# Fused sparse attention and two-of-four expert attention: four-quarter strided values, long-run loads, another split of the tokens, projections of the first batch in parts, other shifts of the steps

## Chip, core and metric

The kernel runs on one core of one Trainium2 chip, as one program that is launched once. The metric is device time in microseconds (us). Before the change the median of 3 runs was 509.25 us (508.88 to 509.28).

## What is computed

Eight batches of 576 tokens. In a first stage 8 heads of 64 channels attend: heads 0 to 3 to the last 32 tokens ("local"), heads 4 to 7 to all earlier tokens with the same remainder modulo 32 ("strided"; 18 tokens per remainder). The result, 512 channels per token, is the input x of a second stage with four experts, each a causal attention of one head of 64 channels with its own projections; every token takes the two experts (K = 2) with the highest gate logits.

Here `rel` is query minus key position and `stride` is 32.

```python
mask_local = (rel >= 0) & (rel < stride)
mask_strided = (rel >= 0) & (pos[None, :] % stride == pos[:, None] % stride)
...
for e in range(E):
    q = x @ wq[e]
    k = x @ wk[e]
    v = x @ wv[e]
    scores = scale * (q @ k.transpose(0, 2, 1))
    scores = np.where(causal, -1000000000.0, scores)
    ...
    ye = a @ v @ wo[e]
    for kk in range(K):
        mask = topk[:, :, kk] == e
        out += mask[..., None] * w[:, :, kk:kk + 1] * ye
```

## The kernel before

**Stage 1** (`stage1(b, hp)`, once for each batch b and pair of heads hp; hp 0 and 1 are local, 2 and 3 strided). It loads q and k of the pair (`load_qk`: L395 local, L401 strided) and v (`load_v`: L422 and L425 local, L430 and L433 strided), all on SyncE's queue (SP). A strided block g holds 54 tokens, those of three remainders (18 tokens each); there are 10 such blocks and one of 36. TensorE (PE) transposes the blocks (`tp`, L446), multiplies queries by keys (`s`, L475), a softmax runs over VectorE (DVE), GpSimd (POOL) and ScalarE (ACT) (L489 to L511), PE transposes the probabilities (`pt`, L534 local, L536 strided) and multiplies them by the values (`xa`: L560 local, L565 strided). The result is split into a high and a low part in a reduced float format (`xh` L580, `xl` L582), so that a product of float32 precision can be had from three faster matmuls (`split3`).

For the strided values of before, the matmul of head h takes its rows from partitions 64h and its output to partitions 64h: two quarters of the 128 x 128 array are used. For the strided scores the rows follow the head and the output the half hf, so all four quarters are.

**Stage 2**: per batch and pair of experts ep, `project` (L674) makes q and k, `values2` (L621) the values and gate logits, and `attend(b, ep, qk, un, key)` runs twice (un = 0 and 1). Queries are cut into five tiles, the first of 64 tokens and four of 128 (`QT`). Per tile: scores against all keys up to the tile's end (`s2`, L727; the 64-token tile in quarters, L709, against 128 keys), row minimum of the negated scores (`max2`, L738, L712), exponential (`exp2`, L745, L715), scaling by the gate weight (`scale2`, POOL, L768, L762), transposes in blocks of 128 keys (`t2`, L790, L795), copies of those (`t2_out`), the product with the values (`acc`, L826, L815), a split (`oh`, `ol`, L840, L842), and the output projection (`out_tile`, `yp`, L857) and a store (L869). The two 64-token tiles of neighbouring batches share one output tile.

**The order of the work** is made by a list scheduler in the program (`schedule`, L160). Each step is an `op(kind, engine, key, ...)`, with a key that is roughly its wanted time; the table `PRI` adds a shift for the kind, and for the kind in a batch. Of the steps that can start at the same time, the one with the lowest key goes first; for PE a step in another mode (how the array is divided: whole, two row halves, two column halves, quarters) has `MODE_PEN = 5.0` added. Each engine's queue runs in the order that comes out. PSUM's 8 banks and the buffers in SBUF are rings.

Of batch 0's `project`, each step of 12 matmuls reads x of all four pairs of heads, so it follows all of stage 1 of that batch:

```python
op("pj", {"PE": 12 * 0.134}, key + step * u, mm, r=xbufs(b) + wbufs(nm), w=[pj, qk[j, u]], mode=M128)
```

Of the kernel before, what the change touches and what calls it, by code (L numbers as in the profile page):

```python
# [20 lines left out]
def attention_moe_kernel(  # L21
# [28 lines left out]
    QT = [(0, 64), (64, 128), (192, 128), (320, 128), (448, 128)]  # L50
    UNITS = [(0, 320, [0, 1, 2]), (320, 256, [3, 4])]
# [29 lines left out]
    class Ring:  # L81
# [30 lines left out]
        "lo_w": -10.0, "lo_w 0": -8.0, "load_qk": -4.0, "load_qk 0": -6.0, "load_qk 7": 6.0, "load_v": 3.0,  # L112
        "load_v 0": -2.0, "load_v 7": 18.0, "load_w": -1.0, "load_w 0": 6.0, "mask 0": -1.0, "mask 7": 15.0,
# [12 lines left out]
        "yp_out": 18.0, "yp_out 0": -9.0, "yp_out 7": 10.0,  # L126
    }

    def op(kind, eng, key, fn, r=(), w=(), mode=None, npk=0, after=()):
# [3 lines left out]
        o.key = key + PRI.get(kind, 0.0) + PRI.get(f"{kind} {batch[0]}", 0.0)  # L133
# [154 lines left out]
    m_str = const.tile([128, 6, 54], F32, name="m_str")  # L288
    m_cau = const.tile([128, S], F32, name="m_cau")
    m_first = const.tile([128, 128], F32, name="m_first")  # L290
    for m in (m_loc, m_str, m_cau, m_first):
        nc.vector.memset(m, 0.0)
# [9 lines left out]
    for hf in range(2):  # L302
        for sl, off in ((slice(0, 5), 0), (slice(5, 6), 10 if hf else 0)):
            v_ = m_str[64 * hf:64 * hf + 64, sl].rearrange("p i (g u) -> p i g u", u=NJ)
            n_ = sl.stop - sl.start
            keep(v_, [[0, n_], [-NJ, 3], [-1, NJ]], -off, 1)
            keep(v_, [[0, n_], [NJ, 3], [0, NJ]], NJ - 1 + off, -1)
    keep(m_cau[:, S - 128:], [[-1, 128]], 0, 1)
    for hf in range(2):
        keep(m_first[64 * hf:64 * hf + 64], [[-1, 128]], 0, 1)  # L310
# [49 lines left out]

    P2 = [ring(f"p2{t}", [128, 128] if t == 0 else [128, 2, q0 + m], 2) for t, (q0, m) in enumerate(QT)]
    NAT = ring("nat", [128, 11 * 2 * D], 2)
    QKT = ring("qkt", [128, 2, S], 2)
    VR = ring("v1", [128, 9 * 2 * D], 2)
    PL = ring("p1l", [128, 2, 5, 96], 2)
    PSR = fixed("p1s", [128, 6, 2, D], 2, value=lambda t: [t[:, :, h, 54:] for h in range(2)])
# [6 lines left out]
    def stage1(b, hp):  # L373
# [5 lines left out]
        nat = (P2[NT - 1] if b == 0 and local else NAT).new(f"nat_{n}")  # L379
# [6 lines left out]
        def nv():  # L386
            if local:
                t = nat.t.rearrange("p a c -> p (a c)") if b == 0 else nat.t
                return t[:, :9 * 2 * D].rearrange("p (g h d) -> p g h d", h=2, d=D)
            return nat.t.rearrange("p (g h d) -> p g h d", h=2, d=D)  # L390
# [12 lines left out]
        for h in range(2):  # L403
            for src, p0 in ((q, 0), (k, 64)):
                op("load_qk", {"SP": 0.66 if local else 1.15}, (k0 - 30 if b else hp), lambda e, src=src, p0=p0, h=h: load_qk(e, src, p0, h),
                   w=[nat], npk=576)

        def vv():
            if local:
                return vt.t[:96].rearrange("p (g h d) -> p g h d", g=9, h=2)  # L410
            return vt.t[:, :11 * D].rearrange("p (g d) -> p g d", d=D)

        def pv2():
            if local:
                return ptt.t[:96].rearrange("p (h f i c) -> p h f i c", h=2, f=2, i=5)
            return ptt.t[:, :12 * 64].rearrange("p (f i c) -> p f i c", f=2, i=6)

        def load_v(e, h):
# [7 lines left out]
            else:  # L426
                for r in range(3):
                    ap = bass.AP(tensor=base.tensor, offset=base.offset + r * D,
                                 ap=[[STR * D, NJ], [3 * D, 10], [1, D]])
                    dma.dma_start(vv()[64 * h + NJ * r:64 * h + NJ * r + NJ, 0:10, :], ap)  # L430
                ap = bass.AP(tensor=base.tensor, offset=base.offset + 29 * D,
                             ap=[[D, 3], [STR * D, NJ], [1, D]])
                dma.dma_start(vv()[64 * h:64 * h + 54, 10, :], ap)  # L433


        for u, (g0, g1) in enumerate(((0, SPL), (SPL, NG))):
            tp = [RB.new(f"tp{u}{x}_{n}") for x in "qk"]
            ws = [GW if local or g < 10 else 36 for g in range(g0, g1)]
            cn, c0 = sum(ws), g0 * GW

            def tps(e, tp=tp, g0=g0, ws=ws):
                c = 0
                for g, w_ in enumerate(ws, g0):
                    for x in range(2):
                        r = slice(64 * x, 64 * x + w_)
                        nc.tensor.transpose(tp[x].t[:, c:c + w_], nv()[r, g].rearrange("p h d -> p (h d)"),  # L446
                                            ident[r, r])
                    c += w_

            op("tp", {"PE": 0.058 * len(ws) + 0.03}, k0 - 14 + u, tps, r=[nat], w=[*tp, qkt], mode=MR)  # L450
            for x in range(2):
                op("tp_out", either(cn), k0 - 13 + u, lambda e, t_=tp[x], x=x, c0=c0, cn=cn: copy(
                    e, qkt.t[:, x, c0:c0 + cn], t_.t[:, :cn]), r=[tp[x]], w=[qkt])

        for h in range(2):
            op("load_v", {"SP": 1.0 if local else 1.9}, (k0 - 25 if b else 4.0 + hp), lambda e, h=h: load_v(e, h), w=[vt], npk=864 if local else 594)
# [8 lines left out]
        def scores(e):  # L465
            for i in range(ni):
                for hf in range(2):
                    g = i + hf * (ni - 1)
                    if local:
                        q0, c0 = 64 * g, max(64 * g - STR, 0)  # L470
                    else:
                        q0, c0 = (54 * g, 54 * g) if g < 10 else (S - 64, S - 54)
                    for h in range(2):
                        r = slice(64 * h, 64 * h + 64)
                        nc.tensor.matmul(sp[h].t[64 * hf:64 * hf + 64, nk * i:nk * i + nk],  # L475
                                         qkt.t[r, 0, q0:q0 + 64], qkt.t[r, 1, c0:c0 + nk], start=True, stop=True)
# [3 lines left out]
        msk = m_loc if local else m_str  # L480

        def pv():
            return p.t if local else p.t.rearrange("p i h c -> p h i c")[:, :, :, :nk]
# [42 lines left out]
        for u in range(2 if local else 1):  # L526
            pt = [RB.new(f"pt{u}{hf}_{n}") for hf in range(2)]

            def tps2(e, pt=pt, u=u):
                for i in range(ni):  # L530
                    for hf in range(2):
# [3 lines left out]
                        else:  # L535
                            nc.tensor.transpose(pt[hf].t[:, 64 * i:64 * i + 64],  # L536
                                                p.t[r, i].rearrange("p h c -> p (h c)"), ident[r, r])

            op("pt", {"PE": 0.06 * ni + 0.03}, k0 - 2 + 0.5 * u, tps2, r=[p[u]] if local else [p[0], p[1]], w=[*pt, ptt], mode=MR)
            for hf in range(2):  # L540
                def dst(u=u, hf=hf):
                    return (pv2()[:, u, hf] if local else pv2()[:, hf]).rearrange("p i c -> p (i c)")
# [383 lines left out]
```

## Time and profile before

| | |
|---|---|
| median of 3 runs | 509.25 us (508.88 to 509.28) |
| the profiled execution's own time | 508.14 us |
| its span, first to last instruction | 506.4 us |
| PE busy | 487.6 us (96%) |
| DVE, ACT, POOL busy | 342.0, 298.5, 205.5 us |
| mean granted TensorE clock | 0.983 of full speed |
| DMA | 43.53 MB, 133,856 of 138,803 packets under 512 B |

The page gives busy time by engine; a table of stretches gives the same in chosen windows with the granted clock; the chain of waits that ended last gives, for pieces of work on the path, their start and the time until the next piece. Float32 matmuls stand in the trace as two instructions each.

### The profile page before, as it was taken

Reading aid. Unit: us, or ns where it says so; the run is one execution under the profiler, and the core shown is the slowest. Engines: PE = TensorE matmul, PEld = TensorE weight load, DVE = VectorE, ACT = ScalarE, POOL = GpSimd, SP = SyncE. Lnnn points to the kernel's source line nnn. Section 1 sums busy time; section 2 is a strip of 40 time slices with the busy share of each in tenths; the row PEclk is TensorE's granted clock in tenths of the full one; section 3 lists DMA queues with packets and bytes.
Section 4 is the critical chain, followed back from the end, with each engine's and each line's share of the span. In section 5 each row is a group of like instructions: output and inputs, shape, how many; then the busy total and the mean of one; then the engine's idle time right before and its main releaser. Section 6 shows DMA issues by size and latency. Waiting matters only on the chain.

```text
span 506.4 us, 17970 instructions
## 1 busy us (share of the span) xinstructions
PE 487.6 (96%) x7192; PEld 411.9 (81%) x7192; DVE 342.0 (68%) x1033; ACT 298.5 (59%) x831; POOL 205.5 (41%) x257
## 2 busy tenths in 40 slices
PE   4779999999999999999999999999999999999997
PEld 3678887998779987898879987799878888788864
DVE  4764888658685778666786687766687677844460
ACT  2653668647765467645665566754676467744462
POOL 6753456520634244441555135352263415520440
PEclk9769999999999999999999999999999999999999
DMA  7759643512451143611542323531344212100103
GB/s 138 164 112 191 132 94 85 133 27 65 119 132 45 37 101 101 170 35 39 136 107 56 73 64 100 148 83 26 92 124 109 49 24 69 45 22 1 54 33 104
DMA packets 138803, 43.53 MB, mean 86 GB/s; under 512 B 133856, under 2 KB 133856, under 8 KB 138720
## 3 DMA queue, kind: packets, MB, share of 16 engines
q1 hardware_dynamic: 138720, 42.39, 35.4%
q8 instruction: 57, 0.93, 0.8%
q14 instruction: 26, 0.21, 0.1%
HBM read 32.92 MB, written 9.44 MB: 84 GB/s over the span
## 4 chain that ended last, share of the span: by engine, by line
PE 88%; SPq 4%; DVE 2%; DMA 2%; ACT 1%; issue 1%; POOL 1%; POOLq 0%; ACTq 0%; DVEq 0%
PE bank L674 20%; PE bank L621 11%; PE bank L857 11%; PE bank L826 10%; PE bank L727 9%; PE bank L790 6%; PE bank L475 5%; PE bank L565 4%; PE bank L446 4%; PE bank L560 4%; PE bank L534 2%; SPq L395 1%; PE bank L709 1%; DMA nat<-in_k_dram 1%; PE bank L536 1%
## 5 line engine op out<-in xcount | busy, mean ns | idle before, releaser
L768 POOL TENSOR_SCALAR p<-p,st,wt 128x192 f32<-128x192 f32 (+3 forms) x128 | 83.4, 666 | 20.2 <-DVE st L752 16.8
L745 ACT ACTIVATE p<-p,st 128x192 f32<-128x192 f32 (+3 forms) x128 | 78.2, 613 | 15.1 <-DVE st L738 14.9
L275 DVE COPY th<-bank 128x384 f32<-128x384 f32 (+2 forms) x87 | 40.0, 476 | 41.1 <-PE bank L790 30.5
L738 DVE CUSTOM_DVE_ANT_0 p<-bank,m_cau 128x192 f32<-128x192 f32 (+3 forms) x128 | 56.2, 476 | 11.5 <-PE bank L727 10.5
L502 POOL TENSOR_TENSOR p1l<-p1l,st 128x960 f32<-128x960 f32 (+1 forms) x18 | 29.0, 1617 | 84.9 <-DVE st L500 60.7
L826 PE MATMUL bank<-th,vs 128*64 128x256 f32 (+1 forms) x512 | 55.3, 356 | 0.0
L727 PE MATMUL bank<-qk 64*128 64x288 f32 (+3 forms) x320 | 54.9, 444 | 0.0
L275 ACT COPY th<-bank 128x384 f32<-128x384 f32 (+2 forms) x105 | 41.6, 420 | 15.3 <-PE bank L790 8.1
L826 PEld LDWEIGHTS bank<-th,vs 128*64 128x64 f32 x512 | 34.4, 137 | 18.2 <-DVE pt L275 1.3
L790 PEld LDWEIGHTS bank<-ident,p 64*128 64x128 f32 x896 | 37.0, 139 | 14.1 <-issue 5.5
L621 PE MATMUL bank<-wh_v,xh 128*128 128x260 f32 (+1 forms) x160 | 46.6, 291 | 0.0
L790 PE MATMUL bank<-ident,p 64*128 64x64 f32 x896 | 45.8, 228 | 0.6 <-POOL p L768 0.5
L621 PE MATMUL bank<-wl_v,xh 128*128 128x260 f32 (+1 forms) x160 | 45.2, 283 | 0.0
L621 PE MATMUL bank<-wh_v,xl 128*128 128x260 f32 (+1 forms) x160 | 45.0, 281 | 0.0
L275 ACT COPY qkt<-bank 128x252 f32<-128x252 f32 (+3 forms) x106 | 37.3, 409 | 12.1 <-PE bank L446 12.1
L275 ACT COPY qk<-bank 128x288 f32<-128x288 f32 x46 | 18.3, 398 | 44.1 <-PE bank L674 43.8
L511 POOL TENSOR_TENSOR p1l<-p1l,st 128x960 f32<-128x960 f32 (+1 forms) x18 | 29.0, 1618 | 29.3 <-DVE st L509 28.9
L674 PE MATMUL bank<-xh,wh_k 128*128 128x288 f32 x128 | 39.8, 311 | 0.0
L674 PE MATMUL bank<-xh,wh_q 128*128 128x288 f32 x128 | 38.5, 301 | 0.0
L674 PE MATMUL bank<-xl,wh_k 128*128 128x288 f32 x128 | 38.0, 297 | 0.0
L674 PE MATMUL bank<-xh,wl_k 128*128 128x288 f32 x128 | 38.0, 297 | 0.0
L674 PE MATMUL bank<-xh,wl_q 128*128 128x288 f32 x128 | 37.7, 294 | 0.0
(125 smaller groups left out, 1219.9 us busy)
## 6 DMA issues: line engine op xcount, KB each, us to landing
out_dram<-ys SPq DMA_DIRECT2D x32, 256.0 KB
v<-in_v_dram SPq DMA_DIRECT2D x32, 192.0 KB
v<-in_v_dram SPq DMA_DIRECT2D x96, 45.0 KB
nat<-in_q_dram SPq DMA_DIRECT2D x28, 144.0 KB
nat<-in_k_dram SPq DMA_DIRECT2D x28, 144.0 KB
nat<-in_q_dram SPq DMA_DIRECT2D x64, 49.5 KB
nat<-in_k_dram SPq DMA_DIRECT2D x64, 49.5 KB
nat<-in_q_dram SPq DMA_DIRECT2D x32, 45.0 KB
```

The lines of the kernel that those rows point to most:

```text
L275: (nc.scalar.copy if e == "ACT" else nc.vector.tensor_copy)(dst, src)
L502: nc.gpsimd.tensor_tensor(P, P, bc[0], ALU.subtract)
L511: nc.gpsimd.tensor_tensor(P, P, bc[2], ALU.mult)
L621: nc.tensor.matmul(vp.t[:m, :NV], xx.t[:, t0:t0 + m], ww.t[:, kt, :], start=i == 0, stop=i == 11)
L674: nc.tensor.matmul(pj.t[:, :HS], ww.t[:, kt, ep * 128:(ep + 1) * 128], xx.t[:, c], start=i == 0, stop=i == 11)
L727: nc.tensor.matmul(sp[a].t[:, :cn], qk.t[r, 0, q0:q0 + m], qk.t[r, 1, c0:c0 + cn], start=True, stop=True)
L738: lambda e, sp=sp, p=p, a=a, c0=c0, cn=cn, hh=hh, nk=nk, acc_=acc_: nc.vector.tensor_tensor_reduce(out=p.t[:, a, c0:c0 + cn], in0=sp[a].t[ ...
L745: op("exp2", {"ACT": 0.485 + 0.00083 * nk}, k_ + 1, lambda e, p=p, a=a, ci=ci: nc.scalar.activation(p.t[:, a], p.t[:, a], AF.Exp, bias=st. ...
L768: lambda e, p=p, a=a, ci=ci, t=t: nc.gpsimd.tensor_scalar(p.t[:, a], p.t[:, a], st.t[:, 14 + ci + a:15 + ci + a], wt.t[:, t, 2 * ep + a:2 ...
L790: nc.tensor.transpose(tp[hf].t[:, 64 * c:64 * c + 64], p2[t].t[r, a, k0:k0 + 128], ident[r, r])
L826: nc.tensor.matmul(acc.t[o, dst:dst + 128 * nb], vw, x.t[:, c:c + nb, :].rearrange("p c q -> p (c q)"), start=j == 0, stop=j == js[-1], sk ...
L857: nc.tensor.matmul(yp.t[:, :DM], xx.t[:, c0:c0 + 128], ww.t[:, ep, :], start=i == 0, stop=i == 5)
```

## The change

- The strided values use row half x = g // 6 and column half h, so four quarters; all 22 matmuls (44 instructions) form one step that writes two banks. For that the probabilities are laid out so that, of each pair of blocks, the two heads lie in opposite halves.
- Strided block g now holds, of each of three runs of 11 (11, 10) neighbouring remainders, one. So one DMA packet carries 10 or 11 tokens of 64 floats for q and k, and 4, 5 or 6 for v, where it carried one; one DMA loads both heads. Per strided pair 6 DMAs for q and k instead of 12, and 6 for v instead of 8. The q and k blocks are transposed by head, 2 x 6 x 2 transposes instead of 22. x is written by three splits instead of two.
- The four 128-token tiles come first, the 64-token tile last: keys 128, 256, 384, 512 and 576 instead of 64 (128 computed), 192, 320, 448 and 576. The last tile runs in quarters, in two halves of 288 keys. In the product with the values it is a third block of 64 columns beside the 128 of tile 3 (`W1 = 192`).
- Batch 0's projections are cut into four steps of three matmuls, one for each pair of heads.
- `PRI` has a shift for nearly every kind in every batch, up to 168.5 in size (before: up to 20).
- Zero fills of the padding of `nat` and `p24`, another mask (`m_last`) instead of `m_first`, a smaller `m_str`.

```diff
-    QT = [(0, 64), (64, 128), (192, 128), (320, 128), (448, 128)]
-    UNITS = [(0, 320, [0, 1, 2]), (320, 256, [3, 4])]
+    QT = [(0, 128), (128, 128), (256, 128), (384, 128), (512, 64)]
+    UNITS = [[0, 1, 2], [3, 4]]
...
-        "acc": 1.0, "acc 0": 8.0, "acc 7": 2.0, "exp2": 1.0, "exp2 0": 10.0, "exp2 7": -4.0, "exp2_0": 15.0,
...
+        "acc": 13.0, "acc 0": -28.0, "acc 1": 0.5, "acc 2": -13.5, "acc 3": 24.0, "acc 4": 4.0, "acc 5": 8.5,
...
+        "gate4 2": 4.5, "gate4 3": 88.5, "gate4 4": -54.5, "gate4 5": 6.5, "gate4 6": 5.5, "gate4 7": 40.5,
+        "gate5": -47.0, "gate5 0": -2.0, "gate5 1": -168.5, "gate5 2": -61.0, "gate5 3": -33.5,
...
                 for r in range(3):
-                    ni = 11 if r < 2 else 10
-                    ap = bass.AP(tensor=base.tensor, offset=base.offset + r * D,
-                                 ap=[[STR * D, NJ], [3 * D, ni], [1, D]])
-                    nc.sync.dma_start(nv()[p0 + NJ * r:p0 + NJ * r + NJ, 0:ni, h, :], ap)
+                    n_ = (11 if r < 2 else 10) * D
+                    ap = bass.AP(tensor=base.tensor, offset=base.offset + 11 * r * D,
+                                 ap=[[STR * D, NJ], [S * D, 2], [1, n_]])
...
-                            r = slice(64 * h, 64 * h + 54)
-                            nc.tensor.matmul(xa.t[o, c:c + z - a], vv()[r, g, :], pv2()[r, hf, i, a:z],
-                                             start=True, stop=True)
...
+                for s_ in range(6):
+                    for x in range(2):
+                        g = 6 * x + s_
+                        if g > 10:
+                            continue
+                        n_ = 54 if g < 10 else 36
+                        m, b_ = divmod(s_, 2)
+                        r = slice(64 * x, 64 * x + n_)
+                        for h in range(2):
+                            nc.tensor.matmul(xa[x].t[64 * h:64 * h + 64, 54 * s_:54 * s_ + n_], vv()[r, h, s_, :],
+                                             pv2()[r, h ^ b_, b_, m, :n_], start=True, stop=True)
...
+            if b == 0:
+                prev = []
+                for kt in range(KT):
...
+                    prev = [op("pj", {"PE": 3 * 0.134}, key + step * u + 0.1 * kt, part,
...
-    BLK = [[[(0, 1), (0, 2), (1, 1), (1, 2), (2, 2)]],
-           [[(0, 3), (0, 4), (1, 3), (1, 4), (2, 3), (2, 4)], [(3, 3), (3, 4), (4, 4)]]]
+    BLK = [[(0, 0), (0, 1), (0, 2), (1, 1), (1, 2), (2, 2)], [(0, 3), (1, 3), (2, 3), (3, 3)]]
...
+            if t == NT - 1:
+                for hh in range(2):
...
+                            nc.tensor.matmul(sp.t[r, :HS], qk.t[r, 0, q0:q0 + 64], qk.t[r, 1, c0:c0 + HS],
+                                             start=True, stop=True)
...
+        jobs = [(a, BLK[un]) for a in range(2)] + ([("l", [(j, NT - 1) for j in range(NT)])] if un else [])
...
+                    if un == 0:
+                        c0, cn, s0 = 128 * j, 384 - 128 * j, 128 * (0, 3, 5)[j]
+                    else:
+                        c0, cn, s0 = 0, W1 if j < 4 else 64, W1 * j
+                    nc.tensor.matmul(acc.t[o, c0:c0 + cn], vw, th[a].t[:, s0:s0 + cn],
```

## Rows read from the trace of the kernel before

**Rows 1.** The page, part 1: busy time and share of the span by engine.

```profile
PE 487.6 (96%) x7192; PEld 411.9 (81%) x7192; DVE 342.0 (68%) x1033; ACT 298.5 (59%) x831; POOL 205.5 (41%) x257
```

**Rows 2.** Busy time in three stretches: window, length, five engines, granted clock, DMA share.

```profile
0.00:53.00 53.00, 39.39 (x633) 35.02 (x634) 30.33 (x78) 24.51 (x64) 29.68 (x50) 0.84 0.75 151
53.00:468.00 415.00, 414.21 (x6256) 351.33 (x6257) 296.63 (x897) 256.08 (x718) 164.35 (x189) 1.00 0.33 80
468.00:507.00 39.00, 34.05 (x308) 25.57 (x306) 15.04 (x58) 17.91 (x49) 11.42 (x19) 1.00 0.18 62
```

**Rows 3.** PE's waits by what released it: total us, times, longest.

```profile
PE bank L446 <- POOL m_first L284: 6.0, 1, 6.0
...
PE bank L790 <- POOL p L768: 0.5, 1, 0.5
```

**Rows 4.** The chain of waits, 112 to 171 us: start, us until the next.

```profile
118.89 1.80 PE bank L727 x12
...
121.89 0.85 PE bank L475 x48
...
127.51 0.80 PE bank L446 x22
128.31 0.36 PE bank L709 x4
...
130.28 0.46 PE bank L790 x10
130.73 0.06 PE bank L795 x2
130.79 0.38 PE bank L727 x4
131.17 0.31 PE bank L790 x10
...
133.93 0.27 PE bank L815 x4
134.19 1.08 PE bank L826 x12
135.28 0.52 PE bank L790 x12
135.79 0.59 PE bank L727 x4
136.39 0.18 PE bank L790 x6
...
140.77 2.10 PE bank L826 x20
...
147.07 1.41 PE bank L565 x44
```

**Rows 5.** The first stretch in parts, columns as in Rows 2.

```profile
0.00:6.00 6.00, 0.04 (x1) 0.07 (x1) 2.46 (x12) 1.28 (x1) 4.84 (x17) 1.00 0.57 123
...
26.00:31.00 5.00, 3.13 (x59) 2.66 (x61) 3.90 (x11) 3.94 (x12) 4.33 (x7) 0.78 0.39 83
31.00:37.00 6.00, 5.39 (x95) 5.09 (x91) 3.19 (x8) 2.42 (x6) 1.49 (x3) 0.50 0.55 123
```

**Rows 6.** The timeline of PE in the first 40 us.

```profile
21.19 1.54 PE L475 MATMUL bank<-qkt 64*64 64x54 f32 x48
...
34.47 2.63 PE L565 MATMUL bank<-pt,v 54*64 54x54 f32 x44 [0.61 <-ACT pt L275]
37.03 0.61 PE L674 MATMUL bank<-xh,wh_k 128*128 128x288 f32 x1
```

**Rows 7.** The timeline of SP, DVE and POOL in the first 14 us.

```profile
2.50 0.32 DVE L260 MEMSET p1s<- 128x60 f32 x4
...
7.76 1.16 SPq L401 DMA_DIRECT2D nat<-in_k_dram  x3
```

**Rows 8.** The timeline of POOL from 200 to 225 us: one unit's scalings.

```profile
213.90 3.04 POOL L768 TENSOR_SCALAR p<-p,st,wt 128x448 f32<-128x448 f32 x4 [0.42 <-DVE st L752]
```

More of the change, by code (lines that the diff above doesn't have):

```diff
@@ L132, in op @@
         o.eng, o.fn, o.mode, o.npk = eng, fn, mode, npk
[L133 removed]
+        o.key = round(key + PRI.get(kind, 0.0) + PRI.get(f"{kind} {batch[0]}", 0.0), 3)
         o.succ, o.ready, o.end = [], 0.0, None
@@ L302, in attention_moe_kernel @@
     for hf in range(2):
[L303 to L307, printed above, removed]
+        v_ = m_str[64 * hf:64 * hf + 64].rearrange("p (g u) -> p g u", u=NJ)
+        keep(v_, [[-NJ, 3], [-1, NJ]], 0, 1)
+        keep(v_, [[NJ, 3], [0, NJ]], NJ - 1, -1)
     keep(m_cau[:, S - 128:], [[-1, 128]], 0, 1)
     for hf in range(2):
-        keep(m_first[64 * hf:64 * hf + 64], [[-1, 128]], 0, 1)
+        keep(m_last[64 * hf:64 * hf + 64, HS - 64:], [[-1, 64]], 0, 1)
     tie = const.tile([128, E, E], F32, name="tie")
@@ L378, in stage1 @@
         k0 = T * (b + 0.25 * hp) if b else 2.0 + 4.0 * hp
-        nat = (P2[NT - 1] if b == 0 and local else NAT).new(f"nat_{n}")
+        nat = (P2[3] if b == 0 and local else NAT).new(f"nat_{n}")
         qkt, st = QKT.new(f"qkt_{n}"), ST1.new(f"st1_{n}")
@@ L451, in stage1 @@
             for x in range(2):
[L452 to L456, printed above, removed]
+                c0 = x * S + 64 * g0 if local else (2 * x + u) * cn
+                op("tp_out", either(cn), k0 - 13 + u, lambda e, t_=tp[x], c0=c0, cn=cn: copy(
+                    e, qkt.t[:, c0:c0 + cn], t_.t[:, :cn]), r=[tp[x]], w=[qkt])
@@ L459, in stage1 @@
+        for h in range(2 if local else 1):
+            op("load_v", {"SP": 1.0 if local else 2.6}, (k0 - 25 if b else 4.0 + hp), lambda e, h=h: load_v(e, h), w=[vt], npk=864 if local else 700)
         sp = [RB.new(f"s{h}_{n}") for h in range(2)]
@@ L586, in attention_moe_kernel, with split @@
-    VS = fixed("vs", [128, NT, NV], 2, value=lambda t: [t[64:128, 0, :]])
+                op("pt_out", either(pn * ni), k0 - 1.5 + 0.5 * u, lambda e, pt=pt, hf=hf, dst=dst, rows=rows, pn=pn: copy(
+                    e, dst(), pt[hf].t[:rows, :64 * ni].rearrange("p (i c) -> p i c", c=64)[:, :, :pn]), r=[pt[hf]], w=[ptt])
+        def split(xa, key, u, *parts):
+            for u, (s_, x_, n_) in enumerate(parts, u):
+                op("xh", {"ACT": act(n_)}, key, lambda e, s_=s_, x_=x_: nc.scalar.copy(x_(xh.t), s_(xa.t)),
+                   r=[xa], w=[xh[u]])
+                op("xl", {"DVE": dve(n_)}, key + 0.5, lambda e, s_=s_, x_=x_: nc.vector.tensor_sub(
+                    x_(xl.t), s_(xa.t), x_(f(xh.t))), r=[xa, xh[u]], w=[xl[u]])
@@ L604, in xbufs @@
     def xbufs(b):
-        return [X[b, kt][i][u] for kt in range(KT) for i in range(2) for u in range(2)]
+        return [X[b, kt][i][u] for kt in range(KT) for i in range(2) for u in range(3)]
     def wbufs(nm):
@@ new lines, in attend, with mm @@
+            sp = [RB.new(f"s2_{n}_{t}_{a}") for a in range(2)]
+            def mm(e, sp=sp, q0=q0, nk=nk):
+                for a in range(2):
+                    r = slice(64 * a, 64 * a + 64)
+                    nc.tensor.matmul(sp[a].t[:, :nk], qk.t[r, 0, q0:q0 + 128], qk.t[r, 1, :nk], start=True, stop=True)
+            op("s2", {"PE": nk * 4 / 2400 + 0.02}, k_, mm,
+               r=[qk[0, u] for u in us] + [qk[1, u] for u in range((nk - 1) // HS + 1)],
+               w=[*sp, p[0], p[1]], mode=MR)
@@ new lines, in attend @@
+            for a in range(2):
+                op("max2", {"DVE": 0.23 + 0.00102 * nk}, k_ + 0.5,
+                   lambda e, sp=sp, p=p, a=a, nk=nk, ci=ci: nc.vector.tensor_tensor_reduce(
+                       out=p.t[:, a, :nk], in0=sp[a].t[:, :nk], in1=m_cau[:, S - nk:], scale=-SCALE, scalar=BIG,
+                       op0=ALU.add, op1=ALU.min, accum_out=st.t[:, ci + a:ci + a + 1]),
+                   r=[sp[a]], w=[p[a], st[t, a]])
+            for a in range(2):
+                op("exp2", {"ACT": 0.485 + 0.00083 * nk}, k_ + 1, lambda e, p=p, a=a, ci=ci, nk=nk: nc.scalar.activation(
+                    p.t[:, a, :nk], p.t[:, a, :nk], AF.Exp, bias=st.t[:, ci + a:ci + a + 1], scale=-1.0,
@@ L835, in attend @@
+                    nc.tensor.matmul(acc.t[o, c0:c0 + cn], vw, th[a].t[:, s0:s0 + cn],
+                                     start=j == 0, stop=j == idx[-1], skip_group_check=True)
+        cols = {0: 768, 1: 4 * W1 + 64}[un]
+        dsts = [O[b, ep]] + ([OF[b // 2, ep]] if un else [])
+        op("acc", {"PE": cols * 4 / 2400 + 0.1}, kk + 4.5, av, r=[vs[j] for j in range(idx[-1] + 1)] + th,
            w=[acc] + [y[un if i == 0 else b % 2] for i, pair in enumerate(dsts) for y in pair], mode=MC)
-        parts = [(O[b, ep], un, 256 * un, 64 - 64 * un, 256)]
@@ L846, in out_tile @@
     def out_tile(b, t, key):
-        c0 = 0 if t == 0 else 128 * (t - 1)
+        last = t == NT - 1
+        c0 = 0 if last else QT[t][0]
         yp, ys = RB.new(f"yp_{b}_{t}"), YS.new(f"ys_{b}_{t}")
-        src = [OF[b // 2, ep] if t == 0 else O[b, ep] for ep in range(2)]
-        need = [x[i] for pair in src for x in pair for i in ((0, 1) if t == 0 else (int(t > 2),))]
+        src = [OF[b // 2, ep] if last else O[b, ep] for ep in range(2)]
+        need = [x[i] for pair in src for x in pair for i in ((0, 1) if last else (int(t > 2),))]
         def mm(e):
```

344 lines of the change are left out of this document (163 added, 181 removed), and 75 rows, old and new, of the table PRI.

## The prediction

> **What bounds the kernel now.** I read the busy time by engine first: PE is busy 96% of the span, the next engine, DVE, 68% [rows 1]. A share over the span can hide stages, so the table of stretches comes next. From 53 to 468 us PE is busy 414.21 of 415 us at the full granted clock, while DVE has 296.63 and DMA a share of 0.33 [rows 2]: there nothing but PE's own work sets the time. PE's waits agree: the longest is 6.0 us at the very start, and the largest one behind POOL's scalings is 0.5 us, once [rows 3]. The two ends are different. In the first 53 us PE is busy 39.39 us at a mean clock of 0.84, in the last 39 us it is busy 34.05 [rows 2]. So the change is to be priced by what it takes from PE's stream, and apart from that at the start.
>
> **Prices.** The chain of waits gives pieces of PE's stream with the time until the next piece, so pipelining is in them. Score pieces of 192 and 320 columns (both heads, two instructions each) last 0.38 and 0.59 us: (0.59 - 0.38) / 128 = 1.64 ns for a column [rows 4]. Ten transposes behind work in another mode last 0.46 us, ten behind work in their own mode 0.31 us [rows 4]: a change of mode costs about 0.15 us.
>
> **Strided values.** 44 instructions in two quarters last 1.41 us, 32 ns each. The strided scores have the same shape (64 x 64, 54 columns) in four quarters: 48 in 0.85 us, 17.7 ns each [rows 4]. 44 x 17.7 ns = 0.78 us, so 0.63 us less per strided pair. From both sides: nothing, if the quarters did not overlap, and 0.70 us if the time were halved. I take the scores' row, since the order there (each row half with both column halves) and the banks (one for each row half) are those of the change. The split of the first bank now waits for all 44 instead of the first 24, but 24/44 of 1.41 is 0.77 us: it starts when it did.
>
> A rule of the Trainium skill speaks against this. TensorE: Matmul & The Clock Gate, section "Wait — 56ns, not 53.3ns?", has it that matmuls start no closer than about 25 ns however few columns they have. By it the 44 would take 1.10 us (an estimate from that page's figure), and the sum below would be 4.3 us smaller. The scores' row, 17.7 ns, is against it for quarters; as a rival it stands below, worked out from rows.
>
> **Strided transposes.** 22 take 0.80 us, 36 ns each [rows 4]; 24 instead: +0.07 us. Together a strided pair saves 0.56 us. There are two per batch; the seven later batches' 14 lie where PE is the bound: 14 x 0.56 = **7.8 us**.
>
> **The other split of the tokens**, for each batch and pair of experts (16 of them), all on PE:
> - Scores. Before 0.36 + 0.38 + 0.59 + 1.80 = 3.13 us for 128 + 192 + 320 + (448 + 2 x 288) = 1664 columns [rows 4]. After 128 + 256 + 384 + 512 + 576 = 1856: 192 more, x 1.64 ns = +0.32 us. The last tile has two pieces in quarters where there was one, which may cost no change of mode or one (0.15): +0.40 us, between 0.32 and 0.47.
> - Transposes. Before 0.46 + 0.06 + 0.31 + 2 x (0.52 + 0.18) = 2.23 us for 58, of which one change of mode is 0.15, so 36 ns each [rows 4]. After 24 + 16 + 10 = 50: -0.28 us.
> - Product with the values. Before 0.27 + 1.08 + 2.10 us for 64 + 640 + 1152 columns [rows 4]; after 768 and 832. 256 columns fewer are 0.42 us; the separate four instructions of the first tile fall away, 0.03 us: -0.45 us.
>
> That is 0.40 - 0.28 - 0.45 = -0.33 us, x 16 = **5.3 us**. The other engines keep about the same sizes (exponentials and scalings of 3200 columns before, 3136 after) and have at least 118 us to spare in the 415 [rows 2], so I cost them at nothing. If that cover were gone, the place would be the transposes behind POOL's scalings, 3.04 us for a unit's four [rows 8].
>
> **Loads.** A strided pair's q and k need 6 DMAs instead of 12, each issue about 1.16 / 3 = 0.39 us of SP's queue [rows 7]; v 6 instead of 8. That is 8 x 0.39 = 3.1 us of SP per pair, and less DMA time, but from 53 us on PE waits for no load, so it is worth nothing there. In batch 0 it puts the weights and batch 1's loads, queued behind, up to 6.2 us earlier. What is late next there is the softmax of the pairs: in the trace the last strided values wait for a copy on ACT, not for a load [rows 6].
>
> **The start.** Batch 0's projections begin at 37.03 us, behind the last strided values (2.63 us, as PE then runs at half its clock) [rows 6]. Three effects:
> - The values in four quarters: the scores' 48 take 1.54 us at that clock [rows 6], so 44 take 1.41: 1.2 us less; for the two pairs, less what falls into gaps, 2.2 us.
> - Projections by pairs: nine of the twelve matmuls of a step no longer need the last pair. From 26 to 37 us PE is idle 1.87 + 0.61 = 2.5 us [rows 5]; filled with such matmuls, that is 2.5 us less to do later. Bounds: 0, if the weights' low parts, made on POOL and DVE in just this stretch, come too late, and 5.7 us if in addition the clock, 0.78 and 0.50 there [rows 5], were full (half of the 6 us at 0.50 and a little more). The parts stand in PE's queue ahead of the last pair's transposes and values; were a part to wait for a weight, those would wait too, up to the 2.5 us again as a loss.
> - The zero fills: eight more at 0.32 / 4 = 0.08 us [rows 7] and a mask of 288 columns, about 0.9 us on DVE, in the first 6 us, in which DVE is busy 2.46 [rows 5]: hidden. If they were not, 0.9 us.
>
> I take **4.7 us** together, between -0.5 and 8.
>
> **The tail** (idle 5 of 39 us [rows 2]) has the same four output tiles behind the last values; I take nothing.
>
> **Sum.** 7.8 + 5.3 + 4.7 = 17.8 us. The profiled execution took 508.14 us (span 506.4 and 1.7 around it): 490.3. The median of the runs is 1.1 us above it: **491.4 us**.
>
> **The rivals.**
> 1. *The quarters overlap in part.* Halfway between 32 and 17.7 ns, 24.9 ns, the 44 take 1.09 us and a pair saves 0.32 - 0.07 = 0.25 us, 3.5 instead of 7.8 in all: **495.7**. For it: the values have 11 blocks, so the last pair of matmuls is alone in its row half, and 54 columns at 1.64 / 2 ns would be 44 ns, so that more than columns counts. Against it: the scores' 17.7 ns. Chance 0.08. The floor of 25 ns of the Trainium skill would give about this time.
> 2. *The quarters don't overlap*, so the change doesn't do what it says: 1.41 us stays and 0.07 is added, 9.8 us of the sum lost at the 14 pairs, less 1 at the start: 491.4 + 8.8 + 1.1 = **501**. It would need a conflict that the scores don't have, such as the values' operands lying in copies of another layout. Chance 0.06.
> 3. *More from the start and fewer changes of mode.* The loads let stage 1 of batch 0 end earlier, the clock rises in it, 8 us instead of 4.7, and the new shifts save 5 changes of mode in a batch (the chain has 17 between 118.89 and 147.07 us, the first and the last of [rows 4], so some 30 in a batch), 40 x 0.15 = 6: **482**. For it: the start's idle time and half clock. Against it: DVE and POOL are busy 3.90 and 4.33 of the 5 us from 26 to 31 [rows 5]. Chance 0.12.
> 4. *The new shifts break up the modes*: slower than before. The shifts are up to 168 where the penalty for another mode is 5, so of PE's waiting steps the key alone decides, and steps of one mode stand less together. Place: PE's stream from 53 to 468 us, which has no slack. Price 0.15 us a change. It cancels the 17.8 us from 119 more changes on, 15 in a batch; with 20 more, **515**. The Trainium skill (TensorEngine Tiling, "Key Properties") also says that a change of mode drains the engine, and the 0.46 against 0.31 us agrees. Against it: the shifts of before, up to 20, also override a penalty of 5, and PE's stream still is dense. Chance 0.10, of which 0.08 ends slower.
>
> **How the numbers follow.** Forecast 0.64; rivals 0.08, 0.06, 0.12 and 0.10 as above. Predicted is the forecast's time, 491.4. The range reaches down to rival 3's 482 and up to 500, which takes in rival 1, a start worth nothing (496.1) and both together; rivals 2 and 4 lie outside, with part of 3: 0.2. 0.2% (1 us) is about what a measurement of this kernel can tell. Faster: 0.64 + 0.08 + 0.06 + 0.12 and nothing of rival 4 = 0.90. Within 0.2%: 0.02, slower: 0.08, both from rival 4.
>
> **What would show it.** In the profile after: the strided values' 44 in about 0.78 us in the chain (1.10 is rival 1, 1.41 rival 2); per pair of experts, the three rows of the product with the values at 0.45 us less, the scores 0.4 more; PE busy some 472 us instead of 487.6, still over 99% in the middle at full clock; the first projections before 33 us. PE's idle time between 53 and 468 us growing past 5 us, or many more ten-transposes pieces at 0.46 us, would make the prediction wrong.

## The result and the profile after

The changed kernel takes **493.29 us** (median of 4 runs, 492.39 to 495.19) against 509.26 (508.88 to 509.52) of the kernel before in the same job: a ratio of 0.969 (0.966 to 0.973). Run once more beside later experiments it took 493.62 us, ratio 0.971 (0.968 to 0.974); its six runs spread over 3.5 us and those of before beside them over 3.9, so the spread, which had been expected to be wider if late loads set part of the time, tells nothing of them. The forecast, 491.4, is 1.9 us too low, and the range held. The profiled run of after took 494.08 us, 14.06 us less than the profiled run of before; its span is 492.4 us (before 506.4). For a profiled run the forecast was 490.3, so there the miss is 3.8 us; the medians are nearer to each other because after's profiled run lies 0.8 us above its median and that of before 1.1 below.

A span is PE's busy time plus PE's idle time. The page's first part for after, which answers to [rows 1]:

```profile
PE 470.0 (95%) x7032; PEld 395.7 (80%) x7032; DVE 318.0 (65%) x1000; ACT 294.4 (60%) x837; POOL 203.9 (41%) x256
```

PE's busy time fell by 487.6 - 470.0 = 17.6 us, and its idle time rose from 18.8 to 22.4 us: 17.6 - 3.6 = 14.0 us of span. Where the idle time is, the table of stretches for after tells (window, length, then PE, PEld, DVE, ACT, POOL busy, granted clock, DMA share, GB/s), against [rows 2]:

```profile
0.00:53.00 53.00, 40.82 (x710) 34.99 (x711) 35.64 (x101) 26.99 (x73) 31.74 (x50) 0.94 0.79 166
53.00:453.00 400.00, 394.42 (x6024) 334.65 (x6023) 268.43 (x850) 248.89 (x715) 161.10 (x189) 1.00 0.31 80
453.00:493.00 40.00, 34.78 (x302) 26.06 (x300) 13.98 (x50) 18.52 (x50) 11.09 (x18) 0.96 0.21 67
```

In the first 53 us PE is idle 12.2 us (before 13.6), at a clock of 0.94 (before 0.84). In the middle it is idle 5.6 us of 400, where it was 0.8 of 415: the stage that had no slack now has waits. The last stretch is as it was (within the span, idle 4.6 us, before 4.4).

The stream itself can be read in the chain of waits for after (start us, us until the next piece), for part of a batch, against [rows 4]:

```profile
117.04 1.12 PE bank L812 x8
...
124.70 1.50 PE bank L832 x12
126.20 0.37 PE bank L886 x12
...
127.58 0.52 PE bank L886 x12
...
129.62 0.40 PE bank L886 x8
130.02 0.91 PE bank L832 x4
130.94 0.24 PE bank L886 x8
131.18 1.45 PE bank L919 x12
132.63 0.46 PE bank L886 x10
...
134.66 1.42 PE bank L919 x20
...
141.10 0.72 PE bank L651 x42
...
145.12 0.15 SPq L460
...
146.78 4.90 DMA nat<-in_k_dram
...
151.82 1.28 PE bank L507 x23
```

L651 is the strided values (the chain's row counts 42 of the 44 matmul instructions of a pair): 0.72 us for 42, where 44 took 1.41. L919 is the product with the values: 1.45 + 1.42 = 2.87 us where it was 0.27 + 1.08 + 2.10 = 3.45. L886 are the transposes, 50 in 0.37 + 0.52 + 0.40 + 0.24 + 0.46 = 1.99 us where 58 took 2.23. L812 and L832 are the scores. And near the end stands what no chain of the middle showed before: a load of strided q and k (L460), on which PE then waits.

The stall in detail, from three views of after: PE's waits by releaser (total us, times, longest), the timeline of SP, and the timeline of PE (start us, us, line; in brackets the idle time ahead), with a matmul of an earlier output projection at full clock as its first line.

```profile
PE bank L507 <- DMA nat<-in_k_dram: 5.5, 5, 2.0
PE bank L507 <- DMA nat<-in_q_dram: 1.6, 2, 0.9
```

```profile
138.95 1.00 SPq L460 DMA_DIRECT2D nat<-in_k_dram  x3
140.18 0.37 SPq L960 DMA_DIRECT2D out_dram<-ys  x1
141.86 3.04 SPq L492 DMA_DIRECT2D v<-in_v_dram  x6
145.00 1.00 SPq L460 DMA_DIRECT2D nat<-in_q_dram  x3
146.10 1.00 SPq L460 DMA_DIRECT2D nat<-in_k_dram  x3
147.20 0.37 SPq L960 DMA_DIRECT2D out_dram<-ys  x1
```

```profile
138.35 0.39 PE L948 MATMUL bank<-wl_o,oh 128*128 128x512 f32 x1
...
151.82 1.28 PE L507 MATMUL bank<-ident,nat 54*128 54x54 f32 x23 [1.96 <-DMA nat<-in_k_dram]
153.03 0.80 PE L948 MATMUL bank<-wh_o,oh 128*128 128x512 f32 x1
153.63 0.63 PE L948 MATMUL bank<-wh_o,ol 128*128 128x512 f32 x1
```

The strided pair's q and k are issued from 145.0 us on: there are two `nat` buffers, the pair that held this one is transposed (L507) up to 145 us, and SP issues six loads of v ahead. They land 4.9 us after the last issue, and PE has nothing else for 1.96 us. From 150 to 156 us the granted clock is 0.72 and an output projection's matmul takes 0.63 us instead of 0.39, as at the lower of the clock's two levels (1.2 and 2.4 GHz). Here one stall is paid twice. In the profile of the second run of after the same place has a wait of 1.06 us, the clock stays at 1.00, and the matmuls of the output projection take 0.39 us:

```profile
150.71 0.92 PE L507 MATMUL bank<-ident,nat 54*128 54x54 f32 x23 [1.06 <-DMA nat<-in_k_dram]
...
151.89 0.39 PE L948 MATMUL bank<-wh_o,ol 128*128 128x512 f32 x1
```

Compared matmul by matmul, the second run gains 2.2 us there on the first, 0.9 of it the shorter wait. So the wait comes back from run to run, the second payment does not.

Before had no such wait, and one number tells why: the time from the last issue of a pair's q and k to the first transpose of that pair. Before, for a pair of the middle (SP, then PE):

```profile
143.41 1.16 SPq L401 DMA_DIRECT2D nat<-in_k_dram  x3
```

```profile
174.44 0.53 PE L446 MATMUL bank<-ident,nat 54*128 54x54 f32 x12
```

From batch 2 on this lead is 21 to 32 us for all twelve strided pairs of before. In after it is 3 to 9 us for ten of the twelve. The load itself hardly changed: the quickest sets past 53 us landed 6.5 us after their first issue in before and 5.9 us in after.

### The profile page after: what moved, and what is told of

It is laid out like the page before. It is cut to its first block, busy times and chain, and to the rows that moved or that the text cites. A ratio compares the mean times of both kernels' runs of the same rounds, so it can differ in the third digit from the quotient of the medians.

```text
span 492.4 us, 17519 instructions
## 1 busy us (share of the span) xinstructions
PE 470.0 (95%) x7032; PEld 395.7 (80%) x7032; DVE 318.0 (65%) x1000; ACT 294.4 (60%) x837; POOL 203.9 (41%) x256
## 4 chain that ended last, share of the span: by engine, by line
PE 78%; DMA 1%; issue 0%; ACT 0%; SPq 0%; ACTq 0%
PE bank L758 18%; PE bank L948 11%; PE bank L705 11%; PE bank L919 8%; PE bank L832 7%; PE bank L886 6%; PE bank L539 4%; PE bank L812 3%; PE bank L507 3%; PE bank L634 3%; PE bank L651 2%; PE bank L597 2%; PE bank L600 1%; DMA nat<-in_k_dram 1%; SPq L460 0%
## 5 line engine op out<-in xcount | busy, mean ns | idle before, releaser
L867 POOL TENSOR_SCALAR p<-p,st,wt 128x128 f32<-128x128 f32 (+3 forms) x128 | 75.9, 607 | 94.7 <-DVE st L851 35.0
L844 ACT ACTIVATE p<-p,st 128x128 f32<-128x128 f32 (+3 forms) x128 | 71.2, 559 | 5.7 <-DVE st L839 5.6
L839 DVE CUSTOM_DVE_ANT_0 p<-bank,m_cau 128x128 f32<-128x128 f32 (+3 forms) x128 | 56.0, 486 | 11.8 <-PE bank L832 10.1
L325 ACT COPY qkt<-bank 128x324 f32<-128x324 f32 (+2 forms) x97 | 36.3, 431 | 23.0 <-PE bank L507 21.8
L919 PE MATMUL bank<-th,vs 128*64 128x192 f32 (+4 forms) x512 | 49.2, 338 | 0.1
L325 DVE COPY th<-bank 128x256 f32<-128x256 f32 (+2 forms) x66 | 31.7, 489 | 24.3 <-PE bank L886 22.6
L325 ACT COPY th<-bank 128x256 f32<-128x256 f32 (+2 forms) x94 | 38.1, 428 | 11.7 <-PE bank L886 9.9
L919 PEld LDWEIGHTS bank<-th,vs 128*64 128x64 f32 x512 | 33.9, 136 | 13.4 <-issue 6.2
L886 PEld LDWEIGHTS bank<-ident,p 64*128 64x128 f32 x800 | 32.2, 138 | 14.9 <-issue 8.8
L832 PE MATMUL bank<-qk 64*128 64x128 f32 (+3 forms) x256 | 43.1, 450 | 0.4 <-ACT qk L325 0.3
L886 PE MATMUL bank<-ident,p 64*128 64x64 f32 x800 | 40.5, 229 | 0.0
L507 PE MATMUL bank<-ident,nat 54*128 54x54 f32 (+1 forms) x636 | 31.3, 236 | 8.9 <-DMA nat<-in_k_dram 5.5
L507 PEld LDWEIGHTS bank<-ident,nat 54*128 54x128 f32 (+1 forms) x636 | 26.2, 148 | 14.0 <-issue 5.0
L539 PE MATMUL bank<-qkt 64*64 64x54 f32 (+1 forms) x1408 | 34.2, 249 | 0.2 <-DVE qkt L325 0.2
L574 POOL TENSOR_TENSOR p1s<-p1s,st 128x648 f32<-128x648 f32 (+1 forms) x18 | 20.7, 1156 | 31.8 <-DVE st L572 19.1
```

Source lines behind the costliest of these rows:

```text
L325: (nc.scalar.copy if e == "ACT" else nc.vector.tensor_copy)(dst, src)
L507: nc.tensor.transpose(tp[x].t[:, w_ * (g - g0):w_ * (g - g0) + w_], blk, ident[r, r])
L539: nc.tensor.matmul(o, lhs, rhs, start=True, stop=True)
L832: nc.tensor.matmul(sp[a].t[:, :nk], qk.t[r, 0, q0:q0 + 128], qk.t[r, 1, :nk], start=True, stop=True)
L839: lambda e, sp=sp, p=p, a=a, nk=nk, ci=ci: nc.vector.tensor_tensor_reduce(out=p.t[:, a, :nk], in0=sp[a].t[:, :nk], in1=m_cau[:, S - nk:], ...
L844: op("exp2", {"ACT": 0.485 + 0.00083 * nk}, k_ + 1, lambda e, p=p, a=a, ci=ci, nk=nk: nc.scalar.activation(p.t[:, a, :nk], p.t[:, a, :nk], ...
```

## The experiments

Three ideas were to be told apart. **Stream**: PE is the bound, so each shorter piece is worth its time whatever the order. **Order**: the new shifts carry the gain, and the shorter pieces become time only in an order made for them. **Loads**: what is missing from the sum went into late loads of strided q and k. All medians stand in this table with the profiled run's PE busy and idle time and granted clock, and the number of times that neighbouring PE steps are of different modes. Each ratio is to before in the same job, where its median was 508.6 to 509.3 us.

| kernel | median us | ratio to before (95%) | PE busy | PE idle | clock | changes of mode |
|---|---|---|---|---|---|---|
| before | 509.26 | 1 | 487.6 | 18.8 | 0.983 | 244 |
| after | 493.29 | 0.969 (0.966 to 0.973) | 470.0 | 22.4 | 0.987 | 245 |
| after, second job | 493.62 | 0.971 (0.968 to 0.974) | 468.6 | 22.8 | 0.999 | 245 |
| e1, row half by row half | 496.88 | 0.979 (0.974 to 0.984) | 476.2 | 23.2 | 0.987 | 245 |
| e7, strided q, k loads left out | 485.57 | 0.954 (0.952 to 0.957) | 464.0 | 19.5 | 0.992 | 245 |
| e6, projections undivided | 506.83 | 0.995 (0.992 to 0.998) | 476.5 | 28.7 | 0.970 | 254 |
| e3, old shifts | 509.91 | 1.000 (0.997 to 1.004) | 482.5 | 26.3 | 0.970 | 275 |
| e8, old shifts, penalty 8 | 513.18 | 1.007 (1.004 to 1.009) | 480.6 | 29.6 | 0.967 | 234 |
| e4, other split alone, old shifts | 516.06 | 1.015 (1.013 to 1.017) | 491.7 | 23.4 | 0.971 | 278 |
| e5, new stage 1 alone, old shifts | 511.08 | 1.006 (1.004 to 1.009) | 487.4 | 21.6 | 0.973 | 266 |
| e11, before with penalty 8 | 516.11 | 1.014 (1.010 to 1.018) | 493.2 | 21.8 | 0.977 | 236 |
| e9, before, no shifts | 524.56 | 1.030 (1.027 to 1.033) | 497.0 | 24.7 | 0.984 | 278 |
| e10, after, no shifts | 515.18 | 1.013 (1.007 to 1.019) | 485.2 | 26.7 | 0.989 | 316 |

**e1: the values by row halves.** Only the order of the 44 within the step changes: the blocks of one row half first, so that two quarters work at a time. Everything else runs in the order of after.

```diff
-                for s_ in range(6):
-                    for x in range(2):
+                for x in range(2):
+                    for s_ in range(6):
                         g = 6 * x + s_
```

> The changed kernel, but the strided values go through one row half of the array first and then through the other, so that only two quarters are at work at a time; instructions, operands and the order of all else are the same. Theory 'stream' (PE's own stream sets the time, each part of the change shortens it by its own amount): the 44 instructions go from about 0.80 back to 1.3 to 1.4 us, 14 pairs in the full stretch x 0.55 to 0.6 = 8 us and 1 at the start: 501 to 503 us. Rival 'order' (the new shifts bring most of the gain, the shorter pieces little): under 497 us.

496.88 us (495.67 to 501.12): 3.3 to 3.6 us above the two medians of after, 4 to 5 by the ratios. That is far below the 501 to 503 of the stream theory and, by 0.1 us, inside the other (under 497). The chain of waits of e1 says that the piece had been sized wrongly:

```profile
145.90 1.08 PE bank L651 x42
```

42 take 1.08 us, 26 ns each, and not the 32 ns of before. Against after's 0.72 for 42 that is 0.36 us a pair, 14 x 0.36 = 5.0 us and two more pairs at the start. So the longer piece does become time of the kernel, for the most part; the four runs spread over 5.5 us, and the profiled one, whose busy and idle time the table has, is the slowest of them (501.12 us). Two row halves at once are worth 0.36 of the some 0.6 us a pair; what in the new layout and step brings the rest was not separated.

**e7: no strided loads after batch 0.** Leaves out the q and k loads of strided pairs in batches 1 to 7, the old values in the buffer are used; order as in after.

```diff
-            else:
+            elif b == 0:
                 for r in range(3):
```

> The changed kernel without the loads of q and k of the strided heads in batches 1 to 7 (the blocks hold what lay there before); every other instruction and the order of each engine are the same. Theory 'late loads' (PE waits for these loads, 1.96 us once at 151.8 us and then runs 3.4 us at half clock, and less at 66.7 us; 4.6 us of the time or more): 487 to 489.5 us, and PE's wait for nat after 60 us gone but for local pairs. Rival 'loads are hidden' (PE would wait there for something else anyway): 492 to 494 us.

485.57 us, 8 us below after and below even the late-loads side. Two stretches of e7 against those of after:

```profile
53.00:112.00 59.00, 58.92 (x977) 50.53 (x978) 42.58 (x130) 40.54 (x117) 27.71 (x30) 1.00 0.29 70
...
53.00:444.00 391.00, 389.52 (x5995) 331.06 (x5995) 267.08 (x847) 245.66 (x707) 158.82 (x187) 1.00 0.24 61
```

PE's idle time from 53 us on falls from 5.6 to 1.5 us. After had, in the first of these stretches,

```profile
53.00:112.00 59.00, 56.84 (x966) 48.15 (x965) 42.93 (x129) 41.20 (x119) 29.99 (x32) 1.00 0.45 105
```

2.2 us idle where e7 has 0.1. In after the waits there are put down to VectorE and ScalarE (1.0 and 0.5 us) as well as to a load (0.6); as all of them go with the loads, the loads were behind them. As the two run in the same order, their matmuls can be compared start by start: e7 gains 2.2 us by 53 us, 2.9 between 53 and 100, 3.4 between 140 and 170 (the stall above) and 0.6 between 370 and 390. So the loads are worth 8 us, 4.1 of it idle time of the middle; busy time is less too (464.0 against 470.0), of which the clock (0.992 against 0.987 of 492 us) bounds 2.5 us. How the loads enter the other busy time, no row says. The edit also takes these loads' traffic away from all other loads, and it was not made to the kernel before, so of the 8 us only the waits are known to be new.

**e6: batch 0's projections undivided.** The four parts become one step of 12 again. The scheduler then orders other steps differently too (254 changes of mode).

> The changed kernel with batch 0's projections undivided, as before; the order shifts with it. Theory 'stream' as predicted (projections by pairs fill 2.5 us of idle time): 495 to 497 us. Rival 'not used' (in the changed kernel the first projection matmul starts at 36.19 us against 37.03 before and the gaps are filled by batch 1's first steps instead): 492 to 495 us.

506.83 us (502.13 to 508.8), far outside both. PE's idle time rises by 6.3 us, 5.3 of it in the first 53 us, and the mean clock falls from 0.987 to 0.970. The timeline of e6 shows the place, to be held against that of after in the part on the start below:

```profile
39.47 1.80 PE L651 MATMUL bank<-pt,v 54*64 54x54 f32 x44 [4.59 <-DVE st L563]
...
43.26 0.61 PE L758 MATMUL bank<-xh,wh_k 128*128 128x288 f32 x1
```

PE waits 4.59 us for the softmax of batch 0's last strided pair, from 37 to 53 us the clock is 0.65 (after 1.00), and the first projection starts at 43.26 us. In after 24 matmuls of the projections' parts fill this wait. So the parts are worth several us at the start, more than the expectation gave them. How much of the 13.5 us is theirs and how much comes of a table made for other steps, this run can't tell, as both changed.

**e3, e4, e5: the old shifts.** e3 is the changed kernel with the table `PRI` of before; e4 has only stage 2 of the change (other split, whole projections), e5 only stage 1 (values, loads, transposes), both with the old table. That table has no entry for the steps of the new last tile (`s2_4`, `max2_4`, `exp2_4`, `scale2_4`), so in e3 and e4 they get no shift. In e3 a part of a projection waits for all three splits of x, as the old shifts may place it before the third:

```diff
-        "acc": 13.0, "acc 0": -28.0, "acc 1": 0.5, "acc 2": -13.5, "acc 3": 24.0, "acc 4": 4.0, "acc 5": 8.5,
+        "acc": 1.0, "acc 0": 8.0, "acc 7": 2.0, "exp2": 1.0, "exp2 0": 10.0, "exp2 7": -4.0, "exp2_0": 15.0,
...
-                               r=[X[b, kt][i][x] for i in range(2) for x in range(2)] + [W[nm][i][kt] for i in range(2)],
+                               r=[X[b, kt][i][x] for i in range(2) for x in range(3)] + [W[nm][i][kt] for i in range(2)],
```

> The changed kernel with the table of shifts of the kernel before (and, so that the order stays free to change, batch 0's projection parts wait for all three splits of x). Theory 'stream': the structure brings most, so 490 to 498 us. Rival 'order': the gain goes with the shifts, 503 to 509 us.

> The kernel before with stage 2 of the changed one alone (the 64-token tile last, in quarters), old stage 1, old shifts, undivided projections. Theory 'stream': 16 x 0.33 to 0.57 us less (predicted 0.33; the changed kernel's own pieces read 0.57) = 500 to 504 us. Rival 'order': no clear change, 507 to 511 us.

> The kernel before with stage 1 of the changed one alone (strided values in four quarters, long-run loads, transposes by head), old stage 2, old shifts. Theory 'stream': 14 x 0.56 = 7.8 us less, and 1 to 2 at the start: 499 to 502 us. Rival 'order': no clear change, 507 to 511 us.

509.91, 516.06 and 511.08 us. The stream theory misses all three; the order theory is near for e3 and e5 (up to 1 us above its range) and 5 us too low for e4. With old shifts the whole change is worth nothing, and each half alone makes the kernel slower. Yet the pieces are as short as in after: the strided values of e3 take 18.2 ns each from 171 to 455 us (after 17.9, before 31.2; mean distance from the start of one to the start of PE's next matmul). Where it went, the stretches of e3 tell:

```profile
0.00:53.00 53.00, 38.54 (x632) 34.03 (x633) 32.63 (x89) 25.10 (x66) 26.51 (x43) 0.77 0.74 166
53.00:112.00 59.00, 55.39 (x992) 47.37 (x992) 44.93 (x132) 37.72 (x108) 28.34 (x30) 0.94 0.36 88
```

A clock of 0.77 and 0.94 against after's 0.94 and 1.00, and 18.1 us idle up to 112 us against 14.3. Of the 16.4 us of span between e3 and after, 30 changes of mode at 0.15 us would be 4.5, idle time is 3.9, and the clock, 0.970 against 0.987 of a span of 509, bounds its part by 8.6. These add up to 17.0, but the largest is a ceiling and not a price: e5 took 510.75 us in a run with a mean clock of 0.973 and 511.24 in one with 1.000, and the second run of after, at 1.00 in the first 53 us where the first had 0.94, was only 0.1 us ahead of it at 45 us. None of the three was changed by itself, so how the 16.4 us divide stays open.

**e8: fewer changes of mode, old shifts.** As e3, with the penalty for another mode at 8; PE's order then has 41 changes less.

```diff
-    MODE_PEN = 5.0
+    MODE_PEN = 8.0
```

> The changed kernel with the shifts of before, as e3_old_shifts (509.9 us), and MODE_PEN 8 instead of 5. PE's order then has 234 changes of mode instead of 275 (after: 245, before: 244). If changes of mode at 0.15 us each are what old shifts cost: 41 x 0.15 = 6.2 us less, 503.7, between 501 and 505.5. If it is where waits and half clock fall, 507 to 513.

513.18 us: no gain from 41 fewer changes, 3.3 us slower instead, and 0.2 us above the range of the other idea. PE's busy time fell by 1.9 us, where 41 changes at 0.15 us would be 6.2, and its idle time rose by 3.3. So the count of changes is not what old shifts cost. Stretches of e8:

```profile
53.00:112.00 59.00, 58.39 (x975) 49.48 (x977) 47.23 (x141) 39.34 (x114) 28.88 (x30) 1.00 0.33 83
112.00:470.00 358.00, 347.51 (x5114) 291.74 (x5110) 234.18 (x731) 207.93 (x600) 133.57 (x158) 0.98 0.29 77
```

The early stretch is now clean, and the waits have moved: 10.5 us idle from 112 us on, at 0.98, where after has 3.4 of 341 us. PE's longest waits in e8 past the start are again for q and k (2.6 and 2.1 us, 7.5 in all from 53 us on), and again four strided pairs have a lead of 1 to 3 us.

**e11, e9, e10: the kernel before in other orders, and both kernels in no special one.** e11 is before with that same penalty of 8; e9 and e10 are before and after with an empty table (`PRI = {}`; in e10 the parts wait as in e3).

> The kernel before, its own shifts, MODE_PEN 8 instead of 5; 236 changes of mode instead of 244. If changes of mode alone count: 8 x 0.15 = 1.2 us less, 508.1. If shifts fit only the rule they were made with: 511 to 517.

> The kernel before with an empty table PRI; 278 changes of mode instead of 244. If the shifts fit the work they were made with and are worth time there too: slower, 34 x 0.15 = 5.1 us for the changes and some us of waits, 514 to 530. If the order hardly matters for the kernel before: 508 to 511.

> The changed kernel with an empty table PRI (its projections' parts wait for all three splits); 316 changes of mode. Neither this nor the kernel before with an empty table has an order made for it. If the shorter stream of PE is worth its 14 us also there: below the kernel before with an empty table by 14 less (316 - 278) x 0.15 = 5.7, so by 6 to 12 us. If the stream is worth nothing without an order of its own: within 3 us of it, or above.

e11: 516.11 us, 7 slower with 8 changes of mode fewer: the table of before loses 7 us under another rule than the one it was made with. e9: 524.56 us, so that table is worth 15 us to the kernel before. e10: 515.18 us, 9.4 below e9, inside the 6 to 12 of the stream theory. This pair is the fairest comparison of the two streams, for neither has an order of its own: PE's busy time is 497.0 and 485.2 us. e10's four runs spread over 5.7 us, so the 9.4 is known to some 3 us. The stream is worth 9.4 us there; with a table for each it is worth 16 (509.3 - 493.3), as the new table gives the new code 515.2 - 493.3 = 22 us where the old one gave the old code 15.

The same pair of kernels settles where the late loads come from. e10 has all pieces of after; what differs is the table (and the wait for the third split). Its lead from the last issue of q and k to the transposes is 32 to 41 us for eleven of the twelve strided pairs from batch 2 on, and from 53 us on PE waits for these loads once, 1.2 us, at the pair with a lead of 2.9 us. So the short leads of after belong to the order that its table makes, and not to the shorter pieces.

## Why the prediction was right, and where it was not

**What bounds the kernel** was read rightly: the gain is PE busy time. The prediction said some 472 us; it is 470.0.

**Strided values.** 44 in 0.78 us was forecast; 42 take 0.69 to 0.90 in the chain, and the mean distance of two is 17.9 ns from 171 to 455 us, as in the scores' row (17.7). A pair saves 44 x (31.2 - 17.9) = 0.59 us there, where 0.63 was forecast. Rivals 1 and 2 (24.9 and 32 ns) fall. (Rival 2's sum is put wrongly: the 14 pairs would lose 14 x 0.63 = 8.8 us, and the 1.1 are lost at the start; its 501 stands. The 4.3 us beside the rule on 25 ns would be 14 x 0.32 = 4.5.) By the Trainium skill (TensorE: Matmul & The Clock Gate, "Wait — 56ns, not 53.3ns?") starts come no closer than about 25 ns; here 42 starts lie in 0.72 us, 17 ns apart, so the measurement decides against that rule for matmuls in four quarters. With two quarters at a time (e1) it is 26 ns.

**The other split.** Product with the values: -0.45 forecast, -0.58 in the chain above. Transposes: -0.28 forecast, -0.24. Scores: +0.40 forecast; 12 in 1.50, 4 in 0.91 and the last tile's 8 in quarters in 1.12 us make 3.53 against 3.13: +0.40. The sum is -0.42 in this place against -0.33. These terms held.

**The start** came near its size, in the main by the mechanisms that were named, but not at the time that was named. At 53 us after has 470.0 - 40.8 = 429.2 us of PE's busy time still before it, before had 487.6 - 39.4 = 448.3. That is 19.1 us less, and the pieces forecast for the stream past 53 us are 7.8 + 5.3 = 13.1. Some 6 us are left for the start and whatever else the order does, where 4.7 was forecast. The strided values run at full clock (0.91 us where [rows 6] have 2.63). The first projection begins at 36.19 us and not before 33, yet it stands ahead of the last pair's values, as the prediction had it. Timeline of PE and stretches of after:

```profile
35.35 0.91 PE L651 MATMUL bank<-pt,v 54*64 54x54 f32 x44
36.19 0.40 PE L769 MATMUL bank<-xh,wh_k 128*128 128x288 f32 x1
...
40.52 0.91 PE L651 MATMUL bank<-pt,v 54*64 54x54 f32 x44
```

```profile
26.00:31.00 5.00, 4.49 (x79) 4.17 (x82) 4.13 (x13) 4.11 (x13) 3.12 (x4) 0.50 1.01 205
31.00:37.00 6.00, 6.00 (x180) 5.46 (x172) 4.21 (x10) 4.87 (x17) 3.82 (x7) 0.86 0.70 168
```

The idle time of [rows 5] shrank (1.87 + 0.61 to 0.51 + 0 us), filled by batch 1's local transposes and scores, which the new order pulls forward. The projections' parts fill the next wait instead: 24 of their matmuls run between 36.19 and 40.30 us, while the last pair's probabilities are still being made and transposed. Undivided (e6), PE waits there.

**The loads** are the step that failed: "from 53 us on PE waits for no load, so it is worth nothing there". That was true of the trace of before, in the order of before, where each pair's q and k had 21 to 32 us to land. The change replaces that order. In the new one ten of twelve pairs have 3 to 9 us, for loads that land some 4 to 6 us after the last issue, and the prediction priced the new shifts by changes of mode alone. PE is idle 5.6 us of the middle, past the 5 that the prediction named as a sign of being wrong, and leaving the loads out gives 8 us (e7). That the order does it, e10 shows: same pieces, other table, leads of 32 to 41 us, one wait of 1.2 us. Why the new table leaves so little time was not tested. The scheduler in the program counts a strided pair's q and k as 2 x 700 packets instead of 4 x 576, so it takes them to land sooner than before.

**The numbers** therefore agree in part by luck. PE has 19.1 us less to do from 53 us on, a little more than the 17.8 of the sum, and it is idle 10.2 us there instead of 5.2: 19.1 - 5.0 = 14.1, the 14 us of the span. A part of the 19.1 comes from steps that the prediction left alone. From 171 to 455 us the mean distance to PE's next matmul is 136.1 ns instead of 138.5 for the projections and 123.0 instead of 126.0 for values and gate logits. Within a step it is the same in both kernels (132.5 and 120 ns); what fell is how often a step of another kind follows (behind 21 of 546 projection matmuls instead of 29 of 480). As the changes of mode are 245 and 244 in all, this may stand against more of them elsewhere.

**Rival 4** (shifts break up the modes) did not come in this form: 245 changes of mode against 244. But its lever, the order, was the right one: the chance of 0.10 rested on the shifts suiting the code, which no row of before could show. With shifts that do not, or with none, the same code gives 510 (e3), 513 (e8) or 515 us (e10), and none of these is a gain. In the Trainium skill (TensorEngine Tiling (Array Packing), "Key Properties") a change of mode drains the engine, and 0.15 us is its price in [rows 4]; e8 and e11 show that a count of them doesn't order kernels: fewer changes were slower both times.

What stays open: why PE's busy time depends on the order beyond the changes of mode and the clock. e10 has 71 changes more than after, 10.7 us at 0.15, and a clock no lower, yet its busy time is 15.2 us larger; e9 against before is 9.4 for 34 changes, 5.1. Some 4 us in each have no row. Nor was a remedy for the late loads run, such as an order for the new code that keeps the leads of before.

## What to carry to other kernels

When PE is the bound and 99% dense, price an edit by the pieces it shortens. When the edit also replaces the order, ask again of each load how long before its first use it is issued: "nothing waits for it" holds only for the old order. Where an order is made by a table of shifts, the table belongs to one exact set of steps: here it is worth 15 to 22 us, as much as the whole change, so a change of code with a stale table may show no gain or a loss (e3, e4, e5), and both kernels with no table (e9, e10) show what the code itself is worth. Keep code and table apart when a part is tested by itself, and look at where the waits stand before the table is blamed (e6).

## What the runs showed of the hardware

Matmuls of 64 rows and 54 columns that go round all four quarters start 17.9 ns apart; with the two row halves one after the other, 26 ns (e1); in the old layout, 31 to 32 ns. A wait of 1.96 us on PE was followed by a stretch at half clock (0.72 from 150 to 156 us, 0.63 us for a matmul that takes 0.39 at full clock), so this stall cost more than its length; a wait of 1.06 us at the same place in the second run of after was not (clock 1.00). Six loads of a strided pair's q and k, in packets of 2.5 or 2.8 KB (10 or 11 tokens of 64 floats), were issued in 1.8 us and landed at the quickest 5.9 us after the first issue; the twelve loads of before, with ten times the packets, were issued in 4.4 us and landed after 6.5. A tenth of the packets made the issue shorter and the landing hardly earlier.
